# First eight pairs' causal mask by TensorE matmuls instead of POOL selects, and a new order of the pair run with the turn of the shift taken out of it

## The chip, the cores and the metric

The kernel runs on one core of one Trainium2 chip. The metric is the device time of one execution in microseconds. Before the change the median of 3 runs is 898.09 us (891.0 to 901.85). The core's engines are TensorE (PE), VectorE (DVE), ScalarE (ACT), GpSimd (POOL) and SyncE (SP), which issues all DMAs here.

## The reference

Causal attention with a bias of running sums, then a gated two-layer block with a three-tap convolution along the sequence. All in float32.

```python
# q, k, v: (8, 8, 576, 64); s: (8, 8, 576)
scores = matmul(q, k.T) / sqrt(64)
cum = cumsum(maximum(s, 0), axis=-1)
scores = where(causal, -1e9, scores + minimum(-(cum[:, :, :, None] - cum[:, :, None, :]), 0))
attn = exp(scores - scores.max(-1))
x = (attn / (attn.sum(-1) + 1e-9)) @ v            # heads joined: (8, 576, 512)
h = maximum(x @ w_in, 0)                          # w_in: (512, 1024)
c = cw[0] * h[s - 1] + cw[1] * h[s] + cw[2] * h[s + 1]
out = (h / (1 + exp(-c))) @ w_out                 # w_out: (1024, 512)
```

## The kernel before

The 64 heads are worked as 32 pairs: head 0 of a pair lies on partitions 0 to 63, head 1 on 64 to 127, four pairs make a batch of the block behind it (called MoE here). Every float32 operand of the main matmuls is split in a rounded part (hi) and a rest (lo), so that three fast matmuls make one product.

A pair p goes through these tasks; their names are those of the kernel's `add(...)` calls:

- `qk`, `hi`, `lo`: load of keys and queries, and the split. `dr`: DMA of the bias rows into `ek`.
- `sh{p}.0` to `.3` on PE (L719): scores of hi parts plus bias, queries on partitions, 64-row matmuls, the two heads in the two halves of the array. They serve the row maxima only. Each part fills two PSUM banks, one for each head.
- `mx` on DVE (L734): adds the mask tile and takes the row maximum of a bank; 12 of them for a pair. They free the banks of `sh`.
- `tn` (L750): TensorE turns the table of maxima, `rt` (ACT) copies it, `ds` (two DMAs) puts it as one more row into `eq`. This is the shift that is subtracted from the scores.
- `sc{p}.0` to `.3` on PE (L795): scores again, keys on partitions, three split products and one matmul (L795, `ek` and `eq`) with bias and shift, all accumulated in PSUM (k = 0 to 3), 64-row matmuls as in `sh`. Two banks a part.
- `ex` on ACT (L810): the exponential by a sigmoid table, from PSUM into `pt`; it frees the banks of `sc`.
- `mk` on POOL (L823): a select that zeroes what lies above the diagonal in each diagonal tile of `pt`: ten for a pair (five tiles, two heads).
- `sum{p}` on PE (L865): row sums with a one-hot operand in 32-column tiles; `pv{p}` (L847): the product with v, in 64-column tiles, into a PSUM tile of its own.
- `inv` (DVE, L884 and L885): reciprocal of the sums; `ri`, `rb`: store it and broadcast it back by DMA; `nm` (DVE, L907): normalise; `xh`, `xl`: split the result into x for the MoE.

MoE tasks: `h` (12 matmuls, L956), `re` (ACT, L968), `ce` (ACT, L980), `ta` (two taps, DVE, L994), `ga` (gate, ACT, L1007), `mu` (DVE, L1013), `uh` and `ul` (split), `o` (six matmuls, L1050), `oe` (copy out), `st` (store).

PSUM gives `pv` two banks and six banks to all others. The weights are loaded and converted during the first pairs, on DVE, ACT and POOL.

The order of the instructions on every engine is not written out by hand. A planner (`Sched.play`) goes through all tasks with costs, tags and pools, and emits them in the order in which it would start them; each engine then runs its queue in that order, and semaphores do the waiting. For PE the planner knows tiling modes: a task of the last mode is preferred by `STAY`. Tasks of a burst are held together: once a burst has begun, PE takes nothing else until it is done. From pair `B0` = 8 on, the PE tasks of a pair form a burst in the order of `ORDER`, and the first task of the burst waits for everything that the others need (`note`, `link`). In burst n stand `tn`, `sc` of pair n, `sum` and `pv` of pair n - 1, and `sh` of pair n + 1:

```python
ORDER = ("tn", "sum", "pv", "sh0", "sh1", "sc0", "sh2", "sc1", "sh3", "sc2", "sc3")
```

Between two bursts PE runs MoE tasks. Before pair 8 there are no bursts and the planner mixes the tasks by their tags.

## Time and profile before

| what | value |
|---|---|
| median of 3 runs | 898.09 us |
| the profiled execution | 900.18 us |
| its span, first to last instruction | 898.3 us |
| mean granted TensorE clock | 0.95 |
| PE busy | 816.2 us (91%), 7973 matmuls |
| DVE busy | 554.8 us (62%) |
| ACT busy | 432.9 us (48%) |
| POOL busy | 328.6 us (37%) |

A row of the profile names the line of the kernel, the engine, the operation, and the tiles that it writes and reads (out<-in). A bracket or a last column gives the idle time ahead of it and whose work ended that. PEld is PE's loading of weights, which runs beside matmuls. Rows of a timeline begin with start and length in microseconds. In a table by stage each row is a stretch of time with its length, the busy time of each engine, the share of full clock granted to TensorE, and the share and rate of the DMA engines.

### The profile page before, as it was taken

What the parts mean: (1) busy time and instruction counts of PE and PEld (TensorE: products, weight loads), DVE (VectorE), ACT (ScalarE), POOL (GpSimd) and SP (SyncE); (2) the same over time, 40 slices, a digit from 0 to 9 for tenths busy, and PEclk for the clock granted to TensorE, in tenths of its full rate; (3) what the DMA queues carried; (4) which work ended last, traced back from release to release, by engine and by line L of the source; (5) the groups of instructions that cost most, each with busy time, mean ns of one, the idle gap of its engine ahead of it and who ended that gap; (6) DMA issues with size and microseconds to landing.
All of it is one profiled execution on the core that took longest, in us unless ns stands there. A gap on an engine that the chain in (4) does not pass through costs nothing.

```text
span 898.3 us, 20425 instructions
## 1 busy us (share of the span) xinstructions
PE 816.2 (91%) x7973; PEld 726.2 (81%) x7973; DVE 554.8 (62%) x1400; ACT 432.9 (48%) x958; POOL 328.6 (37%) x484
## 2 busy tenths in 40 slices
PE   2868688888999999999999999999899999999997
PEld 1746567778888889988888879888788888989996
DVE  8676877884757663766648563766537664636441
ACT  3445454644546363635536263635436363645541
POOL 7334444453332343333523343333423243222211
PEclk9988687896999999999999999999999999999998
DMA  6343323322121222122221222122212211110000
GB/s 183 125 122 110 107 84 107 108 78 89 48 82 60 81 65 65 52 81 67 67 66 49 80 66 69 48 80 68 58 57 66 80 41 29 32 47 17 25 28 26
DMA packets 50187, 63.20 MB, mean 70 GB/s; under 512 B 6063, under 2 KB 39151, under 8 KB 50031
## 3 DMA queue, kind: packets, MB, share of 16 engines
q1 hardware_dynamic: 50091, 61.91, 23.0%
q8 instruction: 62, 1.02, 0.5%
q14 instruction: 34, 0.28, 0.1%
HBM read 48.60 MB, written 13.04 MB: 69 GB/s over the span
## 4 chain that ended last, share of the span: by engine, by line
PE 68%; DVE 10%; DMA 9%; issue 2%; SPq 2%; ACT 1%; POOLq 0%; DVEq 0%; ACTq 0%
PE ps L956 23%; PE ps L1050 22%; PE pv L847 8%; PE ps L795 7%; PE ps L865 6%; DMA rb<-ri_d 6%; DVE junk L734 4%; PE ps L719 3%; DMA ri_d<-ri 2%; DVE rb L907 2%; DMA ht<-w_out 1%; SPq L899 1%; DVE ct L994 1%; DVE ri L885 1%; DVE ct L546 0%
## 5 line engine op out<-in xcount | busy, mean ns | idle before, releaser
L810 ACT ACTIVATE pt<-ps,bias_sb 128x288 f32<-128x288 f32 (+4 forms) x384 | 157.2, 480 | 156.7 <-PE ps L795 129.8
L1050 PE MATMUL ps<-u,wo 128*128 128x288 f32 x1536 | 221.4, 301 | 5.9 <-POOL u L1024 2.9
L956 PE MATMUL ps<-x,wi 128*128 128x290 f32 x1536 | 224.4, 304 | 1.1 <-ACT pt L810 1.0
L1050 PEld LDWEIGHTS ps<-u,wo 128*128 128x128 f32 x1536 | 212.3, 192 | 9.1 <-POOL u L1024 4.1
L956 PEld LDWEIGHTS ps<-x,wi 128*128 128x128 f32 x1536 | 215.8, 195 | 3.4 <-ACT pt L810 1.6
L994 DVE SCALAR_TENSOR_TENSOR ct<-ht,cw_sb,ct 128x288 f32<-128x288 f32 (+1 forms) x256 | 143.6, 564 | 101.3 <-ACT ct L980 96.7
L823 POOL TENSOR_SCALAR_AFFINE_SELECT pt<-pt 128x128 f32<-128x128 f32 x320 | 97.4, 321 | 249.1 <-ACT pt L810 241.5
L1024 POOL TENSOR_TENSOR u<-ct,u 128x576 fp32r<-128x576 f32 x64 | 96.5, 1508 | 225.0 <-ACT u L1020 187.3
L734 DVE CUSTOM_DVE_ANT_0 junk<-ps,mask 128x320 bf16<-128x320 f32 (+2 forms) x320 | 137.5, 430 | 61.2 <-PE ps L719 35.8
L795 PE MATMUL ps<-s 64*128 64x288 f32 (+4 forms) x1152 | 141.5, 334 | 29.8 <-DVE r L734 20.2
L795 PEld LDWEIGHTS ps<-s 64*128 64x128 f32 x1152 | 110.5, 204 | 43.6 <-DVE r L734 28.5
L847 PE MATMUL pv<-pt,v 128*64 128x448 f32 (+4 forms) x768 | 95.5, 399 | 0.5 <-DVE rb L907 0.5
L719 PE MATMUL ps<-s 64*128 64x288 f32 (+4 forms) x384 | 81.0, 345 | 14.3 <-DVE r L734 10.2
L968 ACT ACTIVATE ht<-ps 128x289 f32<-128x289 f32 x128 | 52.7, 411 | 76.2 <-PE ps L956 74.8
L847 PEld LDWEIGHTS pv<-pt,v 128*64 128x64 f32 x768 | 51.0, 139 | 43.7 <-issue 31.2
L678 POOL TENSOR_TENSOR s<-raw,s 128x1152 fp32r<-128x1152 f32 x32 | 85.9, 2684 | 0.7 <-ACT s L674 0.7
L1013 DVE TENSOR_TENSOR ct<-ct,ht 128x576 f32<-128x576 f32 x64 | 62.7, 980 | 22.5 <-ACT ct L1007 22.5
L795 PE MATMUL ps<-eq,ek 64*128 64x288 f32 (+4 forms) x384 | 75.6, 322 | 0.0
L719 PEld LDWEIGHTS ps<-s 64*128 64x128 f32 x384 | 50.0, 199 | 29.9 <-DVE r L734 19.6
L980 ACT ACTIVATE ct<-ht,cw_sb 128x288 f32<-128x288 f32 x127 | 68.4, 539 | 5.8
L719 PE MATMUL ps<-ek,eb 64*128 64x288 f32 (+4 forms) x384 | 65.8, 327 | 2.2 <-DMA ek<-bx 2.2
L865 PE MATMUL ps<-pt,onehot 128*32 128x144 f32 (+4 forms) x1792 | 63.0, 276 | 4.3 <-DVE r L734 1.9
(70 smaller groups left out, 662.6 us busy)
## 6 DMA issues: line engine op xcount, KB each, us to landing
raw<-qk SPq DMA_DIRECT2D x32, 576.0 KB
v<-vp SPq DMA_DIRECT2D x32, 320.0 KB
rb<-ri_d SPq DMA_DIRECT2D x64, 144.0 KB
outT<-ob SPq DMA_DIRECT2D x64, 144.0 KB
ht<-w_in SPq DMA_DIRECT2D x16, 256.0 KB
ht<-w_out SPq DMA_DIRECT2D x16, 256.0 KB
ri_d<-ri SPq DMA_DIRECT2D x32, 72.0 KB
rows_d<-bx SPq DMA_DIRECT2D x1, 1215.0 KB
```

The lines of the kernel that those rows point to most:

```text
L678: tt_on(e)(st[:, 0:2, :], R_t[raw.slot], st[:, 2:4, :].bitcast(F32), op=ALU.subtract)
L719: nc.tensor.matmul(dst[j], l, m, start=(k == 0), stop=(k == 1))
L734: nc.vector.tensor_tensor_reduce(out=junk[:, 0 : c1 - c0], in0=bank(pb, o, o + c1 - c0), in1=mask[:, S - w + c0 : S - w + c1], scale=1.0, ...
L795: nc.tensor.matmul(dst[j], l, m, start=(k == 0), stop=(k == 3))
L810: nc.scalar.activation(PT_t[pts[j].slot][0:jt, O_T[t] + c0 : O_T[t] + c1], bank(pb, o, o + c1 - c0)[0:jt], AF.Sigmoid, bias=bias_sb[0:jt, ...
L823: nc.gpsimd.affine_select(out=reg, in_=reg, pattern=[[1, dg]], compare_op=ALU.is_ge, fill=0.0, base=0, channel_multiplier=-1,)
L847: nc.tensor.matmul(pvt[j * D : (j + 1) * D, o0 : o0 + c1 - c0], vt[0:jt, t, j * D : (j + 1) * D], PT_t[pts[j].slot][0:jt, O_T[t] + c0 : O_ ...
L865: nc.tensor.matmul(bank(sb_, o0, o0 + b_ - a_)[32 * g : 32 * g + 32], onehot[:, j, :], src[:, a_ - c0 : b_ - c0], start=t == 0 and j == 0, ...
L956: nc.tensor.matmul(bank(hb, 0, XW), l, r, start=(k == 0), stop=(k == len(seq) - 1))
L994: nc.vector.scalar_tensor_tensor(cc[:, lo:hi], h_[:, sh + lo : sh + hi], cw_sb[:, 3 * f + k : 3 * f + k + 1], cc[:, lo:hi], op0=ALU.mult, ...
L1024: tt_on(e)(uu[:, 1], C_t[ct.slot], uu[:, 0].bitcast(F32), op=ALU.subtract)
L1050: nc.tensor.matmul(bank(pb, 0, HS), l, r, start=(fp == 0 and k == 0), stop=(fp == NF // 2 - 1 and k == len(seq) - 1),)
```

## The change

1. In the scores of pairs 0 to 7, two more matmuls (one for each head) add the mask to the diagonal tile in PSUM, between the third and the fourth step of the accumulation: the mask tile (0 and -1e30, bf16) times a unit matrix in bf16. They use all 128 rows of the array. The ten POOL selects of each of these pairs are gone, so the sums follow the exponentials directly. Pairs 8 to 31 keep the selects.
2. `ORDER` has no `tn`, begins with `sh0`, `sh1`, `sh2`, then `sum`, `pv`, then `sc0`, `sh3`, `sc1`, `sc2`, `sc3`. The first task of the burst now also waits for the shift (`t_shift`) and for the normalisation of two pairs before (`last_nm`).
3. `tn` is a task by itself, outside the bursts, without a tiling mode. The table of maxima is 128 columns wide (zeroed once), so the turn is a full 128x128 matmul.
4. `LO1` and `LO2` are names for numbers that stay as they were (4.0 and 6.0).

```diff
-ORDER = ("tn", "sum", "pv", "sh0", "sh1", "sc0", "sh2", "sc1", "sh3", "sc2", "sc3")
+ORDER = ("sh0", "sh1", "sh2", "sum", "pv", "sc0", "sh3", "sc1", "sc2", "sc3")
...
-    R8_t = [const.tile([P, 2 * NT], F32, name=f"r{i}") for i in range(2)]
+    R8_t = [const.tile([P, P], F32, name=f"r{i}") for i in range(2)]
...
         make_identity(nc, ident)
+        nc.gpsimd.tensor_copy(unit, ident)
...
+        for r8 in R8_t:
+            nc.gpsimd.memset(r8, 0.0)
...
-            nc.tensor.transpose(bank(tb, 0, P)[0 : 2 * NT, :], R8_t[r8.slot], ident)
+            nc.tensor.transpose(bank(tb, 0, P), R8_t[r8.slot], ident)
 
         t_turn = add(f"tn{p}", [("PE", 0.13)], maxima + [t_ident], a_sh + 1, turn, alloc=[tb, rt],
-                     uses=[r8], mode="c32", burst=group(p))
-        note(p, "tn", t_turn, maxima)
+                     uses=[r8])
...
                             nc.tensor.matmul(dst[j], l, m, start=(k == 0), stop=(k == 3))
+                        if k == 2 and c0 == 0 and p < B0:
+                            dg = min(P, cn)
+                            for j in range(2):
+                                nc.tensor.matmul(
+                                    dst[j][:, 0:dg], mask[:, S - P : S], unit[:, 0:dg],
+                                    start=False, stop=False,
+                                )
...
-            note(p, f"sc{i}", t_sc, [t_lo])
+            note(p, f"sc{i}", t_sc, [t_lo, t_shift])
...
-                    if c0 == 0:
+                    if c0 == 0 and p >= B0:
                         t_exp = add(f"mk{p}.{j}.{t}", [("POOL", 0.29, True)], [t_exp],
...
-        note(p + 1, "pv", t_pv, [])
+        note(p + 1, "pv", t_pv, last_nm[:])
...
+        last_nm[:] = [t_norm]
```

The planner puts all queues in a new order. On PE the head of pair 10's burst stood like this before: output matmuls (`o`), the turn, the sums.

```order
1053 L1050 MATMUL ps_65<-u_343,wo 128x288 x6
1054 L1050 MATMUL ps_65<-u_344,wo 128x288 x6
1055 L750 MATMUL ps_66<-ident,r_97 10x128
1056 L865 MATMUL ps_67<-pt_92,onehot 32x144 x4
1057 L865 MATMUL ps_67<-pt_93,onehot 32x144 x4
1058 L865 MATMUL ps_67<-pt_92,onehot 32x16
```

In the changed kernel the same burst begins with six banks of maxima parts (L724, banks `ps_65` to `ps_70`), and the sums (L876) come behind them:

```order
1226 L968 MATMUL ps_66<-x,wi 128x290 x12
1227 L724 MATMUL ps_65<-s_83 128x288
1228 L724 MATMUL ps_67<-s_83 128x288
...
1231 L724 MATMUL ps_68<-s_83 128x288
1232 L724 MATMUL ps_69<-s_83 128x288
...
1235 L724 MATMUL ps_66<-s_83 128x448
1236 L724 MATMUL ps_70<-s_83 128x448
...
1243 L876 MATMUL ps_65<-pt_93,onehot 32x144 x4
```

and the turn (L755) stands behind the last score part (L799), ahead of the MoE matmuls (L968, L1062):

```order
1325 L799 MATMUL ps_67<-eq_87,ek_85 128x192
1326 L799 MATMUL ps_69<-eq_87,ek_85 128x192
1327 L755 MATMUL ps_68<-ident,r_98 128x128
1328 L968 MATMUL ps_70<-x,wi 128x290 x12
1329 L1062 MATMUL ps_65<-u_364,wo 128x288 x6
```

So the turn left the head of the burst, the sums moved behind three maxima parts, and all six banks are taken in the burst's first steps.

On DVE, before, the normalisation of pair 9 (L907) stood among the maxima (L734) of pair 11, behind seven of the twelve:

```order
516 L734 ISA junk,r_97<-ps_66,mask 128x448
517 L734 ISA r_97 128x1
518 L907 TENSOR_TENSOR rb<-pv,rb 128x576
519 L734 ISA junk,r_97<-ps_66,mask 128x64
520 L734 ISA r_97 128x1
521 L734 ISA junk,r_97<-ps_68,mask 128x320
```

In the changed kernel, in the same burst, a product (L1025) and two taps (L1006) stand among the maxima (L739), and the normalisation (L918) behind all of them:

```order
540 L739 ISA r_98 128x1
541 L1025 TENSOR_TENSOR ct_109<-ct_109,ht_106 128x576
542 L1006 SCALAR_TENSOR_TENSOR ct_107<-ht_104,cw_sb,ct_107 128x288
543 L1006 SCALAR_TENSOR_TENSOR ct_107<-ht_104,cw_sb,ct_107 128x287
544 L739 ISA junk,r_98<-ps_67,mask 128x320
...
551 L739 ISA r_98 128x1
552 L918 TENSOR_TENSOR rb<-pv,rb 128x576
553 L679 CAST s_82<-raw_80 128x1152
```

What moved: the normalisation went from the middle of the maxima to their end; in two of four bursts MoE work stands ahead of the last four maxima.

On ACT, before, the cast of x (L921) stood among MoE work:

```order
299 L980 ACTIVATE ct_108<-ht_103,cw_sb 128x288
300 L1020 CAST u_342<-ct_107 128x576
301 L921 CAST x<-rb 128x2x290
302 L968 ACTIVATE ht_103<-ps_65 128x289
303 L980 ACTIVATE ct_108<-ht_103,cw_sb 128x288
304 L757 CAST rt_99<-ps_67 10x128
```

In the changed kernel, in every second burst, it (L933) stands among the exponentials (L821); in the other bursts it is on DVE:

```order
342 L821 ACTIVATE pt_94<-ps_66,bias_sb 128x448
343 L933 CAST x<-rb 128x2x290
344 L821 ACTIVATE pt_94<-ps_66,bias_sb 64x64
345 L821 ACTIVATE pt_93<-ps_67,bias_sb 128x320
...
348 L821 ACTIVATE pt_94<-ps_69,bias_sb 128x192
349 L761 CAST rt_100<-ps_68 10x128
```

So five exponentials and the copy of the turn now stand behind a cast that reads the normalised rows.

More of the change, by code (lines that the diff above doesn't have):

```diff
@@ L28 @@
 NX = (5, 7)
+LO1, LO2 = 4.0, 6.0
 TP = 20.5
@@ L292 @@
     mask = const.tile([P, S], BF16, name="mask")
+    unit = const.tile([P, P], BF16, name="unit")
     onehot = const.tile([P, 2, 32], F32, name="onehot")
@@ L573, in lo @@
             finish_lo(e, parts()[2].bitcast(F32))
-        return add(name + "l", [("POOL", c_pool(n), True), ("DVE", c_tt(n), True, 6.0)], [h], tag,
+        return add(name + "l", [("POOL", c_pool(n), True), ("DVE", c_tt(n), True, LO2)], [h], tag,
                    lo, uses=ws)
@@ L639, in link @@
                 sch.follow(a, c)
-    last_ek, last_v = [None], [None]
+    last_ek, last_v, last_nm = [None], [None], []
     L = NT - 1
@@ L681, in pair @@
                    a_sh - 5, hi, alloc=[sb], uses=[raw])
-        t_lo = add(f"lo{p}", [("POOL", c_pool(2 * S), True), ("DVE", c_tt(2 * S), True, 4.0)],
+        t_lo = add(f"lo{p}", [("POOL", c_pool(2 * S), True), ("DVE", c_tt(2 * S), True, 4.0 if p >= B0 else LO1)],
                    [t_hi], A - 6, lo, uses=[raw, sb])
@@ L795, in sc_mm @@
                             nc.tensor.matmul(dst[j], l, m, start=(k == 0), stop=(k == 3))
+                        if k == 2 and c0 == 0 and p < B0:
[5 more added lines that the diff above has]
+                                )
                     o += cn
             w = sum(c1 - c0 for _, c0, c1 in part)
-            t_sc = add(f"sc{p}.{i}", [("PE", 4 * c_rt(w))], [t_shift, t_lo], A + 0.1 * i,
+            t_sc = add(f"sc{p}.{i}", [("PE", 4 * c_rt(w) + (0 if p >= B0 else 0.6))], [t_ident, t_shift, t_lo], A + 0.1 * i,
                        sc_mm, alloc=pbs + (pts if i == 0 else []), uses=[sb, ek, eq], mode="r",
                        prev=None if p >= B0 else t_sc, burst=group(p))
-            note(p, f"sc{i}", t_sc, [t_lo])
+            note(p, f"sc{i}", t_sc, [t_lo, t_shift])
             for j in range(2):
```

## The prediction

> **What bounds the kernel now.** I read the page, then the busy time by stage, then one burst on TensorE (PE) and VectorE (DVE), then the waits.
>
> ```profile
> PE   2868688888999999999999999999899999999997
> PE 68%; DVE 10%; DMA 9%; issue 2%; SPq 2%; ACT 1%; POOLq 0%; DVEq 0%; ACTq 0%
> 20.00:226.00 206.00, 167.48 (x1591) 139.29 (x1590) 150.81 (x441) 100.12 (x235) 86.43 (x139) 0.83 0.35 104
> 226.00:757.00 531.00, 513.79 (x5234) 459.73 (x5232) 325.33 (x820) 259.51 (x577) 196.58 (x284) 0.99 0.21 64
> ```
>
> The digits are PE's busy tenths, the second line splits the chain that ended last, and the last two give span, then PE, PEld, DVE, ACT and POOL busy, granted clock and DMA. From 226 us on PE is busy 513.79 of 531 us: what shortens the time there is PE work or PE stalls and nothing else. The first 226 us differ: PE is busy 167.48 of 206 us at a mean clock of 0.83.
>
> A nearly full PE can still be stalled, since a matmul's modelled end hides short waits. So I look at one burst (pair 10) by the starts of its matmuls:
>
> ```profile
> 250.73 0.27 PE L750 MATMUL ps<-ident,r 128*10 128x128 f32 x1
> 250.93 1.82 PE L865 MATMUL ps<-pt,onehot 128*32 128x144 f32 x56
> 252.68 2.92 PE L847 MATMUL pv<-pt,v 128*64 128x128 f32 x24
> 255.53 0.40 PE L719 MATMUL ps<-s 64*128 64x288 f32 x2
> ...
> 256.17 0.56 PE L795 MATMUL ps<-s 64*128 64x288 f32 x6
> ...
> 256.69 0.39 PE L719 MATMUL ps<-s 64*128 64x448 f32 x1
> 257.26 0.47 PE L719 MATMUL ps<-s 64*128 64x448 f32 x1 [0.17 <-DVE r L734]
> ...
> 257.93 0.67 PE L795 MATMUL ps<-s 64*128 64x288 f32 x6
> ...
> 258.60 0.41 PE L719 MATMUL ps<-s 64*128 64x320 f32 x2
> ...
> 259.08 0.27 PE L719 MATMUL ps<-ek,eb 64*128 64x192 f32 x2
> 259.64 0.87 PE L795 MATMUL ps<-s 64*128 64x448 f32 x6 [0.29 <-DVE r L734]
> ...
> 260.81 0.28 PE L795 MATMUL ps<-eq,ek 64*128 64x64 f32 x2
> 261.32 0.70 PE L795 MATMUL ps<-s 64*128 64x320 f32 x6 [0.23 <-DVE r L734]
> ...
> 262.52 0.66 PE L1050 MATMUL ps<-u,wo 128*128 128x288 f32 x3
> ```
>
> Turn, sums (L865), PV (L847), then the maxima parts sh (L719) and score parts sc (L795), then MoE at 262.52. Three starts are late: 257.26, 259.64 and 261.32. What they wait for is DVE, which empties the banks of the maxima parts one after the other, with the normalisation (L907) in between:
>
> ```profile
> 256.10 0.46 DVE L734 CUSTOM_DVE_ANT_0 junk<-ps,mask 128x288 bf16<-128x288 f32 x1 [1.91 <-PE ps L719]
> ...
> 260.37 0.76 DVE L907 TENSOR_TENSOR rb<-pv,rb 128x576 f32<-128x576 f32 x1
> ...
> 263.02 0.36 DVE L734 CUSTOM_DVE_ANT_0 junk<-ps,mask 128x192 bf16<-128x192 f32 x1
> ```
>
> So the burst is paced by 7.3 us of maxima (256.10 to 263.38) that start only when PV is done, while during 4.6 us of sums and PV (250.93 to 255.53) no bank is being filled.
>
> **How much a burst loses.**
>
> ```profile
> 226.32:756.96 530.64, 142.81 (x986) 137.12 (x984) 0.99 0.21 64
> 226.32:756.96 530.64, 145.76 (x1032) 140.82 (x1032) 0.99 0.21 64
> 290.45 9.60 PE ps L1050 x72
> PEld ps L795 <- DVE r L734: 18.0, 35, 1.6
> PEld ps L719 <- DVE r L734: 8.7, 21, 0.5
> ```
>
> From pair 9's turn (226.32) to pair 30's (756.96) lie 21 bursts and their MoE work. MoE: 986 + 1032 matmuls at 9.60 / 72 = 0.133 us is 269 us. The other 262 us are 12.45 us a burst; less turn 0.20, sums 1.75 and PV 2.85 that leaves 7.65 us for sh and sc. Without waits, from the burst's starts: sh0 and sh1 0.64, sc0 0.52, sh2 0.67, sc1 0.67, sh3 0.59 (0.48 and a last step of 0.11), sc2 1.28, sc3 1.20: 5.57 us. So 2.1 us of a burst are stall. The profile itself names (18.0 + 8.7) / 21 = 1.3 us of it as weight loads waiting for DVE; the rest is bursts that ran after a late normalisation, and short clock drops.
>
> **The change part by part.**
>
> *Pair run.* sh0, sh1, sh2 now come first and take all six banks; DVE empties them while PE does sums and PV; then sc0, sh3, sc1, sc2, sc3. I lay that out with the rows above, time 0 at sh0's start. Sums need one bank: the first maximum ends at 256.56 - 255.53 = 1.03, sums come at 0.64 + 0.67 = 1.3: no wait. PV ends near 6; by then the eight maxima of sh0 to sh2 and the reciprocal (1.05, L885) are through DVE. sc0, sh3, sc1 find six free banks. sc2 needs sc0's banks back from ACT:
>
> ```profile
> 256.95 0.89 ACT L810 ACTIVATE pt<-ps,bias_sb 128x288 f32<-128x288 f32 x2 [5.43 <-PE ps L795]
> L968 ACT ACTIVATE ht<-ps 128x289 f32<-128x289 f32 x128 | 52.7, 411 | 76.2 <-PE ps L956 74.8 <-DVE ct L994 0.6
> L1013 DVE TENSOR_TENSOR ct<-ct,ht 128x576 f32<-128x576 f32 x64 | 62.7, 980 | 22.5 <-ACT ct L1007 22.5
> L994 DVE SCALAR_TENSOR_TENSOR ct<-ht,cw_sb,ct 128x288 f32<-128x288 f32 x128 | 68.7, 541 | 47.5 <-ACT ct L980 45.1
> L921 ACT CAST x<-rb 128x580 fp32r<-128x580 f32 x31 | 21.0, 677 | 24.2 <-DVE rb L907 23.8
> L885 DVE RECIPROCAL ri<-rs 128x144 f32<-128x144 f32 x32 | 33.7, 1053 | 1.1
> ```
>
> Exponentials began 0.78 us after sc0 and two took 0.89, so the banks are free 1.67 after sc0's start; sc2 comes 0.63 + 0.59 + 0.67 = 1.9 after it: no wait. If everything fits, all 2.1 us go. Against that stand:
> - One more change between row-tiled and other matmuls in each burst (MoE to sh, sh to sums, where it was turn to sums). Price from PV to sh: the start 0.15 after a 64-column matmul that takes 0.03, and a first step of 0.24 instead of 0.13: 0.23 us. The Trainium skill (TensorEngine Tiling (Array Packing), Key Properties) says that a change of tiling mode drains TensorE. The row agrees; the page gives no figure, so it changes no sum, but it speaks against this change, here and in the masks.
> - sh2 needs the last two banks, one of which the last MoE matmuls before the burst hold until ACT has emptied it (0.41, L968, behind other work): 0.1 to 0.4 us.
> - In two of four bursts the new order puts a gate or a cast among ACT's exponentials and a product and two taps (0.98 + 2 x 0.54 = 2.1 us) on DVE ahead of sh3's maxima. sc3, due 0.29 after its banks are free (1.9 + 1.28 against 1.22 + 1.67), then waits 0.68 - 0.29 = 0.4; the turn behind it needs those maxima, which DVE ends near 10.9 with the turn due near 10.5: another 0.4.
> Together 0.3 + (0.4 + 0.4) / 2 = 0.7 us of new waits, from 0.2 (all fits) to 1.4 (both in every burst). Net gain 2.1 - 0.23 - 0.7 = 1.2 us a burst; 22 bursts (pairs 9 to 30): **-26 us**, from -37 to -10.
>
> *Turn.* It leaves the burst's head for the place behind sc3 and is a full 128x128 matmul, so it needs no tiling change towards MoE. Its copy and the DMA of the shift now have the whole MoE stretch ahead of their reader, so nothing waits for them. What waits behind it on PE, if DVE is late with sh3's maxima, is that stretch. Taken as 0.20 as before, its wait counted above.
>
> *Normalisation.* It stands behind all maxima on DVE. What queues behind its wait for the broadcast DMA is now casts and taps with an MoE stretch of slack; without that cover it costs what the first rival says. The planner also moves 15 of the 32 casts of x from ACT to DVE, which has the room (325.33 of 531 us busy). SyncE's queue has the shift's DMAs behind the broadcast now, not ahead of it, so its wait for the turn holds up output stores and loads alone.
>
> *Masks.* Removed: 80 selects on POOL:
>
> ```profile
> L823 POOL TENSOR_SCALAR_AFFINE_SELECT pt<-pt 128x128 f32<-128x128 f32 x256 | 85.0, 341 | 248.0 <-ACT pt L810 240.5 <-PE ps L795 1.6 <-POOL pt L823 0.4
> PE ps L865 <- POOL pt L823: 0.7, 1, 0.7
> ```
>
> That is at most 80 x 0.341 = 27 us of an engine that is 42% busy in that stage, and PE waited 0.7 us for it: gain 1 at most. Added on PE: 40 places of two 128-column matmuls between row-tiled steps. No row shows such a place. Its lower bound is two extra steps alone (0.06 each, an estimate by proportion to 0.13 for 288 columns): 0.12 us. Its upper bound adds two changes of tiling at 0.23: 0.58 us. I take 0.58, since PV to sh is a change of the same kind: 40 x 0.58 = 23 us of PE, 28 at clock 0.83. How much lies on the path:
>
> ```profile
> by line: DMA rb<-ri_d 10.8%; PE ps L956 9.8%; PE ps L865 5.5%; DMA ht<-w_out 5.5%; DMA ri_d<-ri 5.3%; PE ps L795 4.7%; issue 4.0%; PE pv L847 3.3%; PE ps L1050 3.0%; PE ps L719 2.4%; DVE junk L734 2.4%; SPq L899 2.2%; DVE ct L546 2.2%; DVE
> 204.16 1.69 PE L795 MATMUL ps<-s 64*128 64x288 f32 x6 [4.21 <-DVE r L734]
> 201.80:218.90 17.10, 14.12 (x81) 12.88 (x82) 8.98 (x33) 7.24 (x18) 7.80 (x13) 0.50 0.24 74
> ```
>
> PE's lines are 29% of that stage's chain, DMAs and DVE most of the rest: 0.29 x 28 = **+8 us**. What moves the other way: four hidden-layer and four output tasks (4 x 12 x 0.133 + 4 x 6 x 0.133 = 9.6 us) now run ahead of pair 8's burst, which starts with its shift already there. Before, that burst lost 4.21 us to a normalisation on DVE, and 14.12 us of PE work ran at half clock, some 7 us. I take 8 of these 11 back, not all, since the stage keeps other stalls. First stage: **0**, from -12 (the masks free, all 11 and POOL's 1 back) to +12 (28 x 0.7 on the path, 8 back). The wider maxima tile, its two memsets and the copy of the identity are POOL work of under 1 us before pair 0's scores at 28.8.
>
> *Tail.* Behind PV of pair 31 only seven output tasks of six matmuls (7 x 6 x 0.133 = 5.6 us) now stand before a matmul that reads that pair's normalised rows; before there were 17 tasks.
>
> ```profile
> 529.59 2.75 DMA ri_d<-ri
> 533.12 3.10 DMA rb<-ri_d
> 822.19 1.66 DVE x L925
> ```
>
> From the sums' end to x ready: reciprocal 1.05, store 2.75, 0.78 between the two DMAs, broadcast 3.10, normalisation 0.76, cast 0.68, rest 1.66: 10.8 us. Cover is 2.85 + 5.6 = 8.5: **+2.3 us**.
>
> Sum against the profiled execution, 900.18 (its span of 898.3 and 1.9 around it): 900.2 - 26 + 0 + 2.3 = 876.5. The median of the runs shown, 898.09, lies 2.1 lower: **874 us**.
>
> **The rivals.**
> - *A new wait takes the old one's place.* In every second burst ACT's cast of x stands among the exponentials and waits for the normalisation, thus for the broadcast DMA; four banks are held until then, and the next MoE tasks have two. For it: ACT's cast waits for the normalisation already (23.8 us in its row). Against it: the third bank is first needed some 5 us after the burst (one hidden-layer and four output tasks). Price 11 bursts x (0.76 + 0.68) = 16: **890**. Chance 0.18.
> - *The first stage warms up.* If the new matmuls and the moved MoE work fill the gaps, up to 206 x (1 - 0.83) = 35 us of PE time is saved; with a third of that, 12: **862**. Chance 0.13. The Trainium skill (TensorE: Matmul & The Clock Gate, Part 1) says that the clock halves after an idle window of about 3.4 us; the 4.21 us gap before 204.16 with 0.50 from 201.8 on agrees.
> - *Slower: masks on the path.* If PE paces the first eight pairs and runs them at 0.5, the masks cost 40 x 0.58 x 2 = 46 us instead of 8. From 32 us on the whole gain is eaten. Here 874 + 38 = **912**, or 925 if the pair run gains only half. Against it: DVE and DMA hold the larger part of that chain. Chance 0.08.
> - That the edit does nothing is out: the order shows it on every pair.
>
> **How the numbers follow.** Forecast 0.58 (864 to 884), new wait 0.18, warm 0.13, slower 0.08, others 0.03. Two per cent, about what a measurement here can tell from no change, is 880.1 below and 916 above. Of the forecast about three quarters lie under 880: 0.44, with 0.13 and 0.03 of the new wait: faster 0.60; slower by over 2% half of its case and some of the others, 0.07; within, 0.33. Range: the ends of the terms, -37 - 12 and -10 + 12, with the tail, would reach 851 to 902; leaving out 2 in 10, **854 to 897**.
>
> **What would show it.** Right: a burst near 11.2 us instead of 12.45, PEld's waits for DVE in 226:757 under 10 us, DVE's maxima running beside sums and PV. Wrong: the turn or sc3 waiting over 1 us on DVE or ACT, MoE matmuls waiting for banks behind ACT's cast of x, or a stage before 226 us that grows by more than 12 us with PE on its chain.

## The result: 864.0 us, ratio 0.9629 [0.9566, 0.9692]

The changed kernel takes 864.0 us (median of 4 runs, 861.88 to 865.21), beside 897.75 us for the kernel before in the same comparison. A second comparison (e11 below) gave 867.4 us and a ratio of 0.9689 [0.9618, 0.9760]. So the change makes the kernel 3.1 to 3.7% faster; 874 was forecast. The profiled execution took 865.21 us, its span is 863.5.

First the page of the changed kernel: PE in tenths, the granted clock, and the chain that ended last, by engine.

```profile
PE   2989998889999989999999999999999999999997
...
PEclk9996789979999999999999999999999999999998
...
PE 75%; DVE 9%; issue 4%; DMA 4%; POOL 3%; ACT 3%; SPq 1%; POOLq 0%; DVEq 0%; ACTq 0%
```

Then its two stages (columns as before: span, PE, PEld, DVE, ACT and POOL busy with their counts, granted clock, DMA share and rate).

```profile
20.00:226.00 206.00, 187.28 (x1722) 149.04 (x1723) 152.02 (x446) 101.55 (x236) 71.33 (x64) 0.88 0.33 100
226.00:757.00 531.00, 517.96 (x5483) 474.92 (x5483) 350.45 (x884) 262.65 (x594) 191.40 (x285) 1.00 0.22 67
```

From 226 us on PE is busy 517.96 us instead of 513.79, with 5483 matmuls instead of 5234. In the first stage it is busy 187.28 instead of 167.48 us, at a clock of 0.88 instead of 0.83, and POOL is 15 us less busy. The chain has lost DMA and gained PE.

The same burst as in the prediction (pair 10), on PE, by the starts of its matmuls (L724 maxima parts, L876 sums, L858 PV, L799 score parts, L755 turn, L968 MoE):

```profile
256.22 0.40 PE L724 MATMUL ps<-s 64*128 64x288 f32 x2
...
256.86 0.40 PE L724 MATMUL ps<-s 64*128 64x448 f32 x2
...
258.60 1.83 PE L876 MATMUL ps<-pt,onehot 128*32 128x144 f32 x56 [1.00 <-DVE r L739]
260.36 2.92 PE L858 MATMUL pv<-pt,v 128*64 128x128 f32 x24
263.21 0.67 PE L799 MATMUL ps<-s 64*128 64x288 f32 x6
263.71 0.29 PE L799 MATMUL ps<-eq,ek 64*128 64x288 f32 x2
263.84 0.31 PE L724 MATMUL ps<-s 64*128 64x320 f32 x2
...
267.45 0.33 PE L755 MATMUL ps<-ident,r 128*128 128x128 f32 x1
267.54 1.73 PE L968 MATMUL ps<-x,wi 128*128 128x290 f32 x11
```

and on DVE (L1006 taps, L739 a maximum, L896 reciprocal, L1025 product):

```profile
254.78 3.30 DVE L1006 SCALAR_TENSOR_TENSOR ct<-ht,cw_sb,ct 128x287 f32<-128x287 f32 x4
258.00 0.45 DVE L739 CUSTOM_DVE_ANT_0 junk<-ps,mask 128x288 bf16<-128x288 f32 x1
...
261.47 1.05 DVE L896 RECIPROCAL ri<-rs 128x144 f32<-128x144 f32 x1
...
263.46 0.75 DVE L1025 TENSOR_TENSOR ct<-ct,ht 128x576 f32<-128x576 f32 x1
264.13 1.14 DVE L1006 SCALAR_TENSOR_TENSOR ct<-ht,cw_sb,ct 128x288 f32<-128x288 f32 x2
265.20 0.48 DVE L739 CUSTOM_DVE_ANT_0 junk<-ps,mask 128x320 bf16<-128x320 f32 x1
```

From the first maxima part to MoE the burst takes 11.32 us, and nothing is late behind PV: sc0 follows PV at 263.21, the turn follows sc3 at 267.45, MoE follows the turn after 0.09. The maxima run beside sums and PV. One start is late, that of the sums, and it is new: 1.00 us. All six banks hold maxima parts, so the sums need the first maximum's bank; and DVE, whose queue runs in order, has four taps of MoE before that maximum, which starts at 258.00, 1.78 behind sh0 (0.57 before the change: 256.10 behind 255.53). By bursts this repeats with a period of four: 10.28, 11.31, 10.35 and 10.76 us, mean 10.68. From the start of the burst to the sums these take 1.30, 2.38, 1.35 and 1.78 us; everything behind PV takes 4.33 to 4.40 in all of them.

The waits on PE, 226 to 757 us (us in total, times, longest):

```profile
PE ps L876 <- DVE r L739: 7.9, 11, 1.0
PE ps L1062 <- POOL u L1036: 3.4, 5, 1.0
PE ps L1062 <- DVE u L1032: 1.8, 2, 1.5
```

The view lists no others. Besides the sums' 7.9 us, output matmuls of MoE wait 5.2 us for the split of u; that wait is new too, since before the change the list of PE's waits in this stage has maxima and exponentials alone. In the list of the weight loads, where L795 and L719 waited 18.0 and 8.7 us for DVE's maxima, no wait for a maximum is left.

To see where the time went I split the span of each profile at the end of pair 8's burst and of pair 30's. Since the kernels run different amounts of MoE work ahead of those points, I add 0.1333 us for each MoE matmul that is still to come.

| profile | first stage, to the end of burst 8 | bursts 9 to 30 | rest |
|---|---|---|---|
| before | 214.8 + 2856 x 0.1333 = 595.5 | 276.2 | 26.6 |
| after | 217.7 + 2784 x 0.1333 = 588.8 | 249.6 | 25.1 |
| after, second profile | 594.5 | 248.1 | 25.4 |

The 22 bursts give 26.6 us (28.1 by the second profile), the first stage 6.7 (1.0), the tail 1.5 (1.2). Two profiles of one kernel differ by 5.7 us in the first stage, so single profiles say little there below 6 us, and for the masks I go by the medians. The 22 bursts scatter less from profile to profile: the three with the old pair run (before, and e1 and e5 below) take 275.0 to 279.9 us there, the five with the new one (the two of the table, e2, e4 and e10) 248.1 to 250.4.

The bursts alone, from first matmul to the MoE matmul behind the last, fall from 266.5 to 235.1 us in total. The stretches of MoE work between them go the other way: beyond 0.1333 us a matmul they take 9.7 us before and 14.5 after (12.9 in the second profile), of which the 5.2 us of waits for u are a part.

### The profile page after: what moved, and what is told of

Read it like the earlier page. It is cut to its first block, busy times and chain, and to the rows that moved or that the text cites. A ratio compares the mean times of both kernels' runs of the same rounds, so it can differ in the third digit from the quotient of the medians.

```text
span 863.5 us, 20407 instructions
## 1 busy us (share of the span) xinstructions
PE 809.3 (94%) x8053; PEld 722.3 (84%) x8053; DVE 558.5 (65%) x1430; ACT 418.2 (48%) x934; POOL 301.3 (35%) x401
## 3 DMA queue, kind: packets, MB, share of 16 engines
q8 instruction: 63, 1.03, 0.5%
## 4 chain that ended last, share of the span: by engine, by line
PE 75%; DVE 9%; issue 4%; DMA 4%; POOL 3%; ACT 3%; SPq 1%; POOLq 0%; DVEq 0%; ACTq 0%
PE ps L1062 22%; PE ps L968 20%; PE ps L799 13%; PE pv L858 9%; PE ps L876 6%; PE ps L724 4%; DVE ct L1006 3%; DVE junk L739 2%; DMA rb<-ri_d 2%; POOL u L1036 1%; DVE ct L1025 1%; DMA ek<-bx 1%; ACT ct L1019 1%; PE ps L803 1%; ACT pt L821 1%
## 5 line engine op out<-in xcount | busy, mean ns | idle before, releaser
L821 ACT ACTIVATE pt<-ps,bias_sb 128x288 f32<-128x288 f32 (+4 forms) x384 | 155.0, 477 | 170.8 <-PE ps L799 166.6
L1062 PE MATMUL ps<-u,wo 128*128 128x288 f32 x1536 | 224.4, 303 | 10.1 <-POOL u L1036 5.9
L1062 PEld LDWEIGHTS ps<-u,wo 128*128 128x128 f32 x1536 | 213.5, 193 | 14.1 <-POOL u L1036 8.7
L968 PE MATMUL ps<-x,wi 128*128 128x290 f32 x1536 | 218.3, 300 | 0.4 <-DVE r L739 0.4
L968 PEld LDWEIGHTS ps<-x,wi 128*128 128x128 f32 x1536 | 212.5, 192 | 1.1 <-DVE r L739 0.8
L1006 DVE SCALAR_TENSOR_TENSOR ct<-ht,cw_sb,ct 128x288 f32<-128x288 f32 (+1 forms) x256 | 155.0, 613 | 81.1 <-ACT ct L992 76.3
L739 DVE CUSTOM_DVE_ANT_0 junk<-ps,mask 128x320 bf16<-128x320 f32 (+2 forms) x320 | 136.2, 425 | 70.9 <-PE ps L724 50.5
L1036 POOL TENSOR_TENSOR u<-ct,u 128x576 fp32r<-128x576 f32 x64 | 92.6, 1447 | 228.8 <-ACT u L1032 209.1
L834 POOL TENSOR_SCALAR_AFFINE_SELECT pt<-pt 128x128 f32<-128x128 f32 x240 | 79.0, 349 | 212.4 <-ACT pt L821 203.8
L799 PE MATMUL ps<-s 64*128 64x288 f32 (+4 forms) x1152 | 131.7, 327 | 10.2 <-DVE r L739 7.1
L799 PEld LDWEIGHTS ps<-s 64*128 64x128 f32 x1152 | 109.7, 201 | 18.5 <-DVE r L739 9.2
L858 PE MATMUL pv<-pt,v 128*64 128x448 f32 (+4 forms) x768 | 93.5, 392 | 0.0
L858 PEld LDWEIGHTS pv<-pt,v 128*64 128x64 f32 x768 | 50.1, 137 | 42.0 <-issue 29.9
L799 PE MATMUL ps<-eq,ek 64*128 64x288 f32 (+4 forms) x384 | 80.6, 339 | 0.1
L1025 DVE TENSOR_TENSOR ct<-ct,ht 128x576 f32<-128x576 f32 x64 | 50.4, 787 | 35.0 <-ACT ct L1019 35.0
L876 PE MATMUL ps<-pt,onehot 128*32 128x144 f32 (+4 forms) x1792 | 63.4, 278 | 9.0 <-DVE r L739 7.9
L724 PE MATMUL ps<-s 64*128 64x288 f32 (+4 forms) x384 | 64.6, 328 | 4.4 <-ACT wo L612 2.4
L876 PEld LDWEIGHTS ps<-pt,onehot 128*32 128x32 f32 x1792 | 56.6, 115 | 14.0 <-POOL u L1036 6.4
L724 PE MATMUL ps<-ek,eb 64*128 64x288 f32 (+4 forms) x384 | 56.6, 318 | 4.0 <-DMA ek<-bx 4.0
```

The lines of the kernel that those rows point to most:

```text
L724: nc.tensor.matmul(dst[j], l, m, start=(k == 0), stop=(k == 1))
L739: nc.vector.tensor_tensor_reduce(out=junk[:, 0 : c1 - c0], in0=bank(pb, o, o + c1 - c0), in1=mask[:, S - w + c0 : S - w + c1], scale=1.0, ...
L799: nc.tensor.matmul(dst[j], l, m, start=(k == 0), stop=(k == 3))
L821: nc.scalar.activation(PT_t[pts[j].slot][0:jt, O_T[t] + c0 : O_T[t] + c1], bank(pb, o, o + c1 - c0)[0:jt], AF.Sigmoid, bias=bias_sb[0:jt, ...
L834: nc.gpsimd.affine_select(out=reg, in_=reg, pattern=[[1, dg]], compare_op=ALU.is_ge, fill=0.0, base=0, channel_multiplier=-1,)
L858: nc.tensor.matmul(pvt[j * D : (j + 1) * D, o0 : o0 + c1 - c0], vt[0:jt, t, j * D : (j + 1) * D], PT_t[pts[j].slot][0:jt, O_T[t] + c0 : O_ ...
```

## The experiments

All ratios are to the kernel before, with 95% intervals; 0.01 is 9 us. Each median is of four runs, in e1, e3 and e5 of ten. The planner orders all queues anew for every edit that changes a task, so most runs differ from the changed kernel in more places than the edit names; e4 alone has the changed kernel's tasks and costs, as e5 has e1's.

| run | what | median us | ratio |
|---|---|---|---|
| e1 | masks on PE, old pair run | 901.2 | 1.0046 [1.0003, 1.0089] |
| e2 | new pair run, selects on POOL | 871.27 | 0.9740 [0.9666, 0.9815] |
| e3 | new pair run, masks on PE in all 32 pairs | 900.78 | 1.0055 [1.0018, 1.0092] |
| e4 | new pair run, first eight pairs without any mask | 859.4 | 0.9605 [0.9526, 0.9685] |
| e5 | old pair run, first eight pairs without any mask | 891.49 | 0.9956 [0.9917, 0.9995] |
| e6 | turn apart, maxima parts behind PV as before | 904.74 | 1.0119 [1.0048, 1.0190] |
| e7 | maxima parts first, turn in the burst | 879.25 | 0.9820 [0.9752, 0.9887] |
| e8 | sh2 behind PV | 871.23 | 0.9719 [0.9640, 0.9798] |
| e9 | sums in the PV tile | 913.35 | 1.0195 [1.0120, 1.0270] |
| e10 | first eight pairs: selects that nobody waits for | 855.17 | 0.9557 [0.9480, 0.9634] |
| e11 | the changed kernel again | 867.4 | 0.9689 [0.9618, 0.9760] |
| e12 | PV in two tiles, sums in the first | 855.25 | 0.9579 [0.9518, 0.9641] |

### One half of the change at a time: e1, e2

e1 keeps the mask matmuls and takes back the rest:

```diff
-ORDER = ("sh0", "sh1", "sh2", "sum", "pv", "sc0", "sh3", "sc1", "sc2", "sc3")
+ORDER = ("tn", "sum", "pv", "sh0", "sh1", "sc0", "sh2", "sc1", "sh3", "sc2", "sc3")
...
-                     uses=[r8])
+                     uses=[r8], mode="c32", burst=group(p))
+        note(p, "tn", t_turn, maxima)
```

> The masks of the first eight pairs on TensorE, with the pair run and the turn as before. If the parts of the change simply add (theory A: the pair run gives about 26 us from pair 9 on, the first stage gives about 7 with the masks in it), this run ends 0 to 8 us under the kernel before: 890 to 898. If the first stage's gain comes from the moved MoE work and the shift being there for pair 8's burst, not from the masks (theory B), the masks alone cost their place on the path: 898 to 910. If the masks pace the early pairs (theory C, the slower rival of the prediction): over 915.

e2 keeps the pair run and the turn, and has the selects in every pair:

```diff
-                        if k == 2 and c0 == 0 and p < B0:
+                        if False:
...
-                    if c0 == 0 and p >= B0:
+                    if c0 == 0:
```

> The new pair run and the turn apart, with the selects on POOL in every pair and no mask matmul. Theory A (the parts add): 26 to 27 us under the kernel before, so 870 to 874, and the change as a whole 5 to 8 us faster than this run. Theory B (the first stage gains by the moved work, the masks cost something): 862 to 866, level with the change or a little under it. Bursts from pair 9 on by both: mean 10.7 us, as in the kernel after.

The pair run alone gives 25 us of the some 30. The masks alone cost some 4. So the parts do not add up: e2 came out as theory A has it and e1 as theory B. On top of the new pair run the masks seem to give 4 to 7 us, by medians, where alone they cost; the intervals of e2 and of the change overlap, so that this last gain is likely and not proven. The next runs go into it. Bursts 9 to 30 take 249.5 us in e2, as in the kernel after, so the pair run's gain doesn't hang on the masks.

### What the masks cost and what the selects cost: e4, e5, e10, e11, e3

e4 leaves out the masking of pairs 0 to 7 altogether:

```diff
-                        if k == 2 and c0 == 0 and p < B0:
+                        if False:
```

> The change, with the 80 mask matmuls of the first eight pairs left out (those pairs are not masked at all). What the masks cost on the path of the first stage is the difference to the kernel after. By the prediction's share (0.29 of 28 us): 8 us less, about 856. If the mask matmuls lie in gaps of TensorE: no difference, 864. If TensorE paces these pairs at the low clock: 20 to 45 us less. If the matmuls keep the clock up, this run is slower than the kernel after.

e5 is the same edit on e1, with the old pair run.

> Pair run and turn as before, and in the first eight pairs neither selects nor mask matmuls (those pairs are not masked at all). With the new pair run, taking the selects out of the first eight pairs without putting anything in their place was worth 11.9 us (871.3 to 859.4). If the selects cost that much in any run (theory A): 12 us under the kernel before, 882 to 887, and the masks then cost the old run the 14 to 19 us up to 901. If the selects cost something only where the pair run is new (theory B): 893 to 898, and the masks cost 3 to 8, as in the new run.

e5's 891.49 lies between its two theories.

e10 is e4 (without the planner's 0.6 us for the masks) with the selects of the first eight pairs kept but written elsewhere, so that the sums don't come behind them:

```diff
-                            out=reg, in_=reg, pattern=[[1, dg]], compare_op=ALU.is_ge, fill=0.0,
+                            out=unit[0:jt, 0:dg] if p < B0 else reg, in_=reg, pattern=[[1, dg]], compare_op=ALU.is_ge, fill=0.0,
...
+                    elif c0 == 0:
+                        add(f"mk{p}.{j}.{t}", [("POOL", 0.29, True)], [t_exp], A + 0.1 * i, sc_mask,
+                            uses=[pts[j]])
```

> The changed kernel without the mask matmuls; in the first eight pairs POOL does its 80 selects as before, reading the exponentials, but writes them to a tile that nobody reads (those pairs are not masked). So POOL has the same work and the same waits, and the sums follow the exponentials directly. With selects that count the new pair run took 871.3, without any 859.4. Theory A (the selects cost because the sums come behind them): 858 to 862. Theory B (they cost because they fill POOL's queue ahead of splits and weight pieces): 868 to 873.

> The changed kernel once more, beside the two others on one chip: 862 to 866. It gives the base for the price of the masks and for the sums' wait.

867.4 lies above that by 1.4; two medians of one kernel differ by 3.4 us here.

With the new pair run, going from selects (0.9740) to no mask (0.9605 and 0.9557) is worth 12 to 16 us; putting the mask matmuls in (0.9629 and 0.9689) takes 2 to 12 of them back. With the old run the selects are worth 4 us (0.9956) and the matmuls cost 8 (1.0046). The cleanest price of the mask matmuls is e4 against the changed kernel and e5 against e1, where no other task changes: by medians 5 to 8 us and 10, by ratios 2 to 8 and 8. So the masks cost about what the prediction said, some 8 us, but the selects that they replace were worth far more than 1.

e10 says which side of the selects it was: POOL still does 80 of them, reading the exponentials, and the run is as fast as with none. POOL's own work isn't the cost; that sums and PV stand behind it, in the run and in the plan, is. The waits of e2 (20 to 205 us; first on POOL, then on PE) show it only in part:

```profile
POOL pt L834 <- ACT pt L821: 40.8, 18, 10.0
```

```profile
PE ps L755 <- DVE r L739: 13.1, 4, 4.1
PE ps L724 <- DVE r L739: 7.3, 3, 6.2
...
PE ps L876 <- POOL pt L834: 3.1, 2, 2.2
```

POOL stands waiting for exponentials for 40.8 us, with the rest of its queue behind, but PE's sums wait 3.1 us for POOL. The other 9 to 13 us are not in that row. They are likely to lie in the order that the planner makes when it sees the sums ready later, in which PE waits elsewhere (13.1 us at the turn and 7.3 at maxima parts, both for maxima; in that stretch of the changed kernel the turn waits for nothing). How the 9 to 13 us are made up of such places wasn't taken apart.

e3 prices a place of the mask where PE is the bound:

```diff
-                        if k == 2 and c0 == 0 and p < B0:
+                        if k == 2 and c0 == 0:
...
-                    if c0 == 0 and p >= B0:
+                    if False:
```

> The change, with the mask added by TensorE in all 32 pairs and no select on POOL at all: 120 more places of two matmuls in pairs 8 to 31, where TensorE is the bound. This prices a place. By the price the prediction took (0.58 us, two changes of tiling): 120 x 0.58 = 70 us over the kernel after, about 934. By its lower bound (0.12, the two steps alone): 14 us over, about 878. POOL's 240 selects go; if the sums had waited for them, up to 2 us less.

900.78 less 865.7 (the mean of the two medians of the changed kernel) is 35 us for 120 places, 0.29 each, with the selects of those pairs gone at the same time. On PE itself a place is a little dearer, as a burst without late sums shows (pair 11 of e3):

```profile
294.07 0.66 PE L799 MATMUL ps<-s 64*128 64x288 f32 x6
294.66 0.28 PE L803 MATMUL ps<-unit,mask 128*128 128x128 bf16 x2
294.88 0.40 PE L799 MATMUL ps<-eq,ek 64*128 64x288 f32 x2
295.11 0.31 PE L724 MATMUL ps<-s 64*128 64x320 f32 x2
```

The mask matmuls (L803) start 0.59 after sc0, where the fourth step would start at 0.50; the fourth step starts at 0.81 and takes 0.23, where it took 0.13 (263.71 to 263.84 in the kernel after): 0.41 us for this place. In bursts without a wait everything behind PV takes 6.25 us in place of 4.38, 0.37 for each of the five places. The late sums come sooner meanwhile (1.54 for 2.38 behind the burst's start in every fourth burst), so over all of bursts 9 to 30 (274.2 us for 235.1) a place costs 0.36. Between the bursts 9 us of stall are gone (5.4 for 14.5 beyond the matmuls' time; no wait for u is left in e3's list), which makes the 0.29. The prediction's bounds, 0.12 and 0.58, hold both; the value it took, the upper one, is too high.

### Order or turn: e6, e7

e6 has the turn apart and the masks, but the old order of the burst:

```diff
-ORDER = ("sh0", "sh1", "sh2", "sum", "pv", "sc0", "sh3", "sc1", "sc2", "sc3")
+ORDER = ("sum", "pv", "sh0", "sh1", "sc0", "sh2", "sc1", "sh3", "sc2", "sc3")
```

> The changed kernel with the old order of the burst less the turn: sums and PV first, maxima parts after them; the turn apart and the masks stay. Theory A (the gain of the pair run is the maxima parts ahead of sums and PV): as the kernel with the masks alone, 898 to 904. Theory B (the turn apart carries a good part of it): 880 to 892. Theory C (the turn behind the last score part now waits for the last maxima, which end about 0.9 us after the last score part in the old order): 22 bursts of 0.9 us on top, 915 to 922.

904.74, just above theory A's range. The old waits of the weight loads are all back (226 to 757 us), and bursts 9 to 30 take 282.1 us:

```profile
PEld ps L799 <- DVE r L739: 21.3, 35, 1.6
...
PEld ps L724 <- DVE r L739: 12.9, 31, 0.4
```

e7 has the new order, with the turn back at the head of the burst; its narrow table, its tiling mode and its place in the burst's tasks come back too (not shown):

```diff
-ORDER = ("sh0", "sh1", "sh2", "sum", "pv", "sc0", "sh3", "sc1", "sc2", "sc3")
+ORDER = ("tn", "sh0", "sh1", "sh2", "sum", "pv", "sc0", "sh3", "sc1", "sc2", "sc3")
```

> The changed kernel with the turn back in the burst, at its head, narrow and in the mode of the sums as before; maxima parts ahead of sums and PV, and the masks, stay. Theory A: one more tiling change and the same bursts, 0.2 to 0.4 us a burst over the changed kernel, 868 to 873. Theory B (the turn apart carries a good part): 880 to 892. If the shift's two DMAs come late for the first score part, 6 us behind the turn, that part waits for DMA and the run lies over 880 for that reason.

879.25, between the theories, and neither the shift nor a tiling change is why. Three of four bursts take 10.55 to 11.08 us, as theory A has it. The fourth takes 14.5 (four times of five; the fifth is told in the last section). First its PE of one such burst, then all engines in the 3.41 us around its wait and in the next 3.41 (columns as in the table by stage above):

```profile
275.16 0.28 PE L724 MATMUL ps<-ek,eb 64*128 64x64 f32 x2
277.81 3.14 PE L877 MATMUL ps<-pt,onehot 128*32 128x144 f32 x56 [2.38 <-DVE r L739]
280.88 3.19 PE L859 MATMUL pv<-pt,v 128*64 128x128 f32 x24
284.00 0.66 PE L800 MATMUL ps<-s 64*128 64x288 f32 x6
```

```profile
274.66:278.07 3.41, 1.03 (x19) 0.92 (x21) 3.19 (x8) 1.89 (x3) 0.00 (x0) 1.00 0.01 2
278.07:281.48 3.41, 3.41 (x62) 3.03 (x55) 2.34 (x10) 0.00 (x0) 1.41 (x1) 0.50 0.02 5
```

DVE's queue has a rest of x (1.84 us), four taps and a product ahead of the first maximum there, so the sums wait 2.38 us, and the granted clock behind it is 0.50 for 3.41 us: the sums take 3.07 in place of 1.76, PV 3.12 in place of 2.85. So the turn's place matters by what the planner puts ahead of the first maximum, and the order of maxima parts, sums and PV carries the gain: 18 of some 27 us in these 22 bursts with the turn in its old place (258.4 us), none of it with the turn moved alone (e6).

### The sums' wait: e8, e9, e12

e8 begins the burst with four banks of maxima, not six:

```diff
-ORDER = ("sh0", "sh1", "sh2", "sum", "pv", "sc0", "sh3", "sc1", "sc2", "sc3")
+ORDER = ("sh0", "sh1", "sum", "pv", "sh2", "sc0", "sh3", "sc1", "sc2", "sc3")
```

> The changed kernel with sh2 behind PV, not ahead of the sums. The sums then need no bank that a maximum has to free first: in the changed kernel they wait 1.0 us in one burst of four and 0.5 us in another, 0.38 on average, 8 us over 22 bursts. Theory A (VectorE has the room: eight maxima, 5 us, in the 5.6 us between PV and the turn): up to 8 us under the changed kernel, 856 to 862. Theory B (the maxima of sh2 and sh3 then hold the banks of sc1 to sc3 as in the kernel before): the wait comes back behind PV, 0.5 to 1 us a burst over, 868 to 880.

The sums' wait is gone (0.72 us from the burst's start in all bursts), but the run takes 871.23: by its size theory B, by its cause neither. Three bursts of four take 10.65. The fourth takes 12.1 to 13.7, because sh3 and sc2 then need banks that exponentials still hold, not maxima; where it takes 13.7, the clock is at half behind these waits:

```profile
280.07 0.42 PE L724 MATMUL ps<-s 64*128 64x320 f32 x2 [0.65 <-ACT pt L821]
...
282.31 1.29 PE L799 MATMUL ps<-s 64*128 64x448 f32 x6 [0.47 <-ACT pt L821]
```

e9 keeps the order and puts the sums into columns of the PV tile that PV doesn't use:

```diff
-        pv, sb_ = buf("pv"), psb()
+        pv = buf("pv")
+        own = p + 1 >= B0
+        sb_ = pv if own else psb()
+        def rows_at(c0, c1):
+            return pvt[:, c0:c1] if own else bank(sb_, c0, c1)
```

> The changed kernel with the row sums of pairs 7 to 31 put into 144 columns of the PV tile that PV doesn't use, not into one of the six banks. The sums then wait for no maximum. Theory A (the bank is what the sums wait for): the 1.0 us and 0.5 us waits of two bursts in four go, 0.38 x 22 = 8 us under the changed kernel, 854 to 858, and every burst takes 10.3 to 10.4 us. Theory B (VectorE is late with its maxima in those bursts whatever the sums do): the same wait comes back at sc0, sh3 or sc1 behind PV, 862 to 866. If PV has to wait for the reciprocal because both stand in one tile: 1.4 us a burst over, 890 or more.

913.35. The sums start 1.30 to 1.35 us into every burst, so the bank was what they waited for. But the reciprocal's first step (L901) reads a tile that PV is still writing, and waits for all of PV, with seven maxima behind it in DVE's queue:

```profile
DVE rs L901 <- PE pv L864: 50.4, 21, 3.2
```

This run shows a third dependency and doesn't decide between the two theories. e12 takes it away: PV's result stands in two tiles, and of the tile with the sums PV writes its first block alone.

```diff
-    pvt = psp.tile([P, 2 * 512], F32, name="pv")
+    pva = psp.tile([P, 512], F32, name="pva")
+    pvb = psp.tile([P, 512], F32, name="pvb")
...
-            nc.vector.tensor_tensor(rb_t, pvt[:, PV0 : PV0 + S], rb_t, op=ALU.mult)
+            nc.vector.tensor_tensor(rb_t[:, 0:P], pva[:, PV0:512], rb_t[:, 0:P], op=ALU.mult)
+            nc.vector.tensor_tensor(rb_t[:, P:S], pvb[:, 0 : S - P], rb_t[:, P:S], op=ALU.mult)
```

> The changed kernel with the PV result in two tiles of one bank each; the row sums of pairs 7 to 31 stand in free columns of the first, of which PV writes only its first block, so the reciprocal waits for two matmuls of PV and not for all of it. The normalisation becomes two products (128 and 448 columns). In the run with the sums in the one PV tile the sums no longer waited (1.3 us from the burst's start to the sums in every burst), but the reciprocal waited 2.3 us for PV with the maxima behind it. Theory A (both waits gone): every burst 10.3 to 10.4 us, 0.38 x 22 = 8 us less than the changed kernel's 864 to 867, so 856 to 860. Theory B (VectorE is late in two of four bursts whatever the sums do): waits of 0.5 to 1 us at the score parts behind PV, 863 to 868. If the reciprocal still waits for all of PV: over 900.

855.25 us, level with e10, which spares the masks. By medians this is 9 to 12 us under the changed kernel, by ratios 5 to 10; the intervals overlap, but all four runs (852.9 to 859.89) are below all eight of the changed kernel (861.88 to 869.86). The size is that of theory A. Pair 10's burst, PE and then DVE (L725, L882, L864, L800, L740 and L1013 are here what L724, L876, L858, L799, L739 and L1006 are in the changed kernel):

```profile
255.94 0.40 PE L725 MATMUL ps<-s 64*128 64x288 f32 x2
...
257.26 1.83 PE L882 MATMUL pva<-pt,onehot 128*32 128x144 f32 x56
259.01 0.44 PE L864 MATMUL pva<-pt,v 128*64 128x128 f32 x4
...
265.66 0.71 PE L800 MATMUL ps<-s 64*128 64x320 f32 x6 [0.32 <-DVE r L740]
...
266.35 0.48 PE L800 MATMUL ps<-s 64*128 64x192 f32 x6
```

```profile
254.50 3.29 DVE L1013 SCALAR_TENSOR_TENSOR ct<-ht,cw_sb,ct 128x287 f32<-128x287 f32 x4
257.71 0.45 DVE L740 CUSTOM_DVE_ANT_0 junk<-ps,mask 128x288 bf16<-128x288 f32 x1
...
260.03 0.30 DVE L901 TENSOR_SCALAR rs<-pva 128x144 f32<-128x144 f32 x1
260.37 1.05 DVE L902 RECIPROCAL ri<-rs 128x144 f32<-128x144 f32 x1
...
263.03 0.75 DVE L1032 TENSOR_TENSOR ct<-ct,ht 128x576 f32<-128x576 f32 x1
263.70 1.10 DVE L1013 SCALAR_TENSOR_TENSOR ct<-ht,cw_sb,ct 128x288 f32<-128x288 f32 x2
264.71 0.48 DVE L740 CUSTOM_DVE_ANT_0 junk<-ps,mask 128x320 bf16<-128x320 f32 x1
```

DVE is as late as before with its first maximum (257.71), and the sums start at 257.26 all the same. The bursts take 10.29, 10.92, 10.36 and 10.33 us. The 0.6 us of the second are in the row of 265.66: a score part that waits for the bank of a maximum behind a product and two taps, which is theory B's wait in one burst of four.

So the sums' wait doesn't make up the whole gain. All waits on PE in this stage are now these:

```profile
PE ps L800 <- DVE r L740: 1.8, 6, 0.3
PE ps L975 <- ACT pt L822: 0.5, 1, 0.5
```

In the measure of the table above, bursts 9 to 30 take 238.9 us, 9 to 11 under the changed kernel's two profiles. The bursts themselves give 4.3 of that (230.8 for 235.1): 0.4 us a burst for the sums, less 0.2 that come back at the score part. The other 5 to 6 lie between the bursts, where the output matmuls' waits for u (5.2 us above) are gone as well. Why these went with the others wasn't taken apart.

## Why the prediction was right, point by point

The profiled executions differ from the sum of 876.5 us by 11.3 (865.21) and 6.7 (869.77). By the table above the terms are: pair run 0.6 and 2.1 better than forecast, first stage 6.7 and 1.0, tail 3.8 and 3.5.

- **Pair run, -26: measured -26.6 and -28.1.** The mechanism is the one given: e6 (order undone) loses all of it, e2 (masks undone) keeps all, e7 (turn back) keeps 18. The experiments change the plan with the order, so they show the order as planned and not the single moves in it. In the measure of the prediction a burst now costs (531.68 - 2125 x 0.1333) / 22 = 11.29 us, with the rows below (span of 22 bursts from 207.42, and the MoE matmuls in it, L968 and L1062); 11.2 was forecast, from 12.45.

```profile
207.42:739.10 531.68, 150.97 (x1069) 147.24 (x1068) 1.00 0.22 67
```

```profile
207.42:739.10 531.68, 150.90 (x1056) 143.92 (x1056) 1.00 0.22 67
```

- **"No wait" for the sums' bank: wrong.** The step took DVE to be idle when the first part's matmuls end (first maximum at 1.03 after sh0's start). In two of four bursts DVE's queue still holds taps; the sums wait 1.0 and 0.5, 0.4 us a burst on average. In e12, without this wait, the 22 bursts take 4.3 us less and the MoE stretches between them another 5 to 6.
- **sc3 and the turn, 0.4 each in two of four bursts: not seen in the changed kernel, seen in e12.** The product and the taps do stand ahead of sh3's maxima, as said (263.46 and 264.13), but the burst was already 1.0 us late by then, which gave DVE the time. With the sums' wait gone, the wait at a score part appears (0.6 in one burst of four). Nor did sh2 wait for its banks (0.1 to 0.4 in the prediction): it starts 0.64 behind sh0, as without a wait. So the 0.7 us of new waits came out as 0.4 by another wait than those named; that the sum was near is luck, by errors that offset each other.
- **Six free banks for sc0, sh3, sc1, and no wait of sc2 on ACT:** right; nothing behind PV is late.
- **One more tiling change, 0.23:** the burst without a wait takes 10.28. Turn 0.09 (in its new place, up to MoE's start), sums 1.75, PV 2.85 and 5.57 for sh and sc make 10.26, so no such price is left to see. Between mask and score parts there is a price (0.37 to 0.41 a place, of which 0.22 are the two matmuls). The Trainium skill (TensorEngine Tiling (Array Packing), Key Properties) says that a change of mode drains TensorE. The 0.09 and 0.10 us around e3's mask matmuls would fit, though these differ in type too; the changed burst shows nothing of it.
- **Masks, +8: 2 to 12 by e4 and e10, 8 by e5 and e1.** A place was taken at 0.58 and measures 0.37 on PE (in pairs 8 to 31, by e3). 40 places at clock 0.88 are then 40 x 0.37 / 0.88 = 17 us of PE; 7, the middle of 2 to 12, is 0.4 of it, where a share of 0.29 was taken. So a price too high and a share too low met near the right product, and within 2 to 12 the share stays open.
- **POOL's selects, "gain 1 at most": wrong, 12 to 16 us in the new run.** The step read the price from PE's wait for POOL (0.7 us), which is only the wait that ended last, in an order that was planned with the selects in it. e10 shows that it is the place of the selects ahead of the sums that costs. In the old run they were worth 4.
- **First stage, 0: -6.7 and -1.0 in two profiles.** The zero is partly luck: its terms came out otherwise. Pair 8's burst took 21.74 us before (193.05 to 214.79, clock 0.70) and takes 10.26 (207.42 to 217.68, clock 1.00, no wait) and 10.25 in the two profiles after, so some 11 us came back there and not 8. The rest of the stage lost 5 to 10 of them. Whether the moved MoE work and the early shift did it, as the prediction has it, stays open: without selects that burst is short in the old run too (12.72 in e5, with less MoE work ahead of it than before), and with them it is long in the new one (20.42 in e2).
- **Tail, +2.3: -1.5 and -1.2.** The chain was summed too long. In the changed kernel's profile pair 31's x is ready 9.1 us after the end of its sums (784.79 to 793.88), not 10.8: the cast, now on DVE, takes 0.47 for 0.68, the rest 0.76 for 1.66, and from the reciprocal's end to the normalisation, with the two DMAs between, it is 5.5 us (786.29 to 791.82) for 6.6. The hidden-layer matmuls behind the seven output tasks start at 793.98, with no gap ahead of them.
- **The rivals.** ACT's cast of x does wait among the exponentials, as the first rival said, but no MoE matmul waits for a bank behind it. The first stage is warmer (0.88 for 0.83), without the 12 us of the second. The slower rival's masks at half clock would have made e4 20 to 45 us faster than the changed kernel; it is 5 to 8.
- **The clock's fall in pair 8's burst.** The prediction took the gap of 4.21 us with 0.50 from 201.8 on as agreeing with a whole idle window. But the gap begins at 199.95, so the half clock comes 1.85 us into it; the last section has more of these.

## What to carry to other kernels

Look for engines whose work could run during another's, and start the producer of the longer chain first: here moving three maxima parts ahead of sums and PV, with the turn out of the burst, was worth some 26 us of about 30, with almost the same instructions; 18 of them came without moving the turn. After such a move read the head of every in-order queue again, because the next wait is at whatever shares a buffer with it; a free corner of another tile (with the tile cut so that no reader waits for a foreign writer) took that wait away too. Count the stretches between the bursts as well: a good part of what e12 and e3 gained or lost stood there. A wait row gives what ended last in one planned order; it doesn't bound what the removal of a dependency is worth.

## What the runs showed of the hardware that was not expected

The half clock came after much less than a whole idle stretch. In the stage from 226 to 760 us of all 14 profiles there are 25 spells at 0.50. Each begins after a 3.41 us stretch in which PE was idle, by its matmuls' records, for 0.9 to 2.4 us; e7's, shown above, with 2.38. No stretch with less than 0.9 us idle is followed by one. Idle time alone doesn't decide it: e9 has 14 stretches with 1.25 to 1.77 us idle and no fall behind them, e7 one with 2.01. The Trainium skill (TensorE: Matmul & The Clock Gate, Part 1) speaks of a whole idle window of about 3.4 us; the length of a window agrees, the idle time that it takes does not. In e7 the spell cost (3.07 - 1.76) + (3.12 - 2.85) = 1.6 us beside the wait of 2.38 itself. The burst with 2.01 confirms the price: its sums start as late as in the other four (4.11 us behind the burst's start), the clock stays at 1.00, and it takes 12.96 us where the others take 14.54 to 14.58.
